# Denominators of two 512-token chunks in one TensorE burst, with reordered multiplications and five early final tiles

## The chip, the cores and the metric

The kernel runs on one core of a Trainium2 chip. The metric is device time in microseconds (us); the runs of one kernel agree within 0.4%.

Comparisons use a *stage length* read from the trace: from the start of the last burst of state products (its first matmul, at 313.99 us of the kernel before) to the start of the last matmul of the kernel.

## The reference

`x` is 2048 tokens of 1024 features. Branch A is linear attention with 32 heads of 32; branch B a dilated sliding-window softmax attention. The result is `g * A + (1 - g) * B`, with one gate `g` per token. What matters here is the end of branch A:

```python
pq, pk = phi(q), phi(k)                       # phi(t) = t+1 if t>0 else exp(t), + 1e-6
kv = einsum("bhsd,bhse->bhde", pk, v)
z = einsum("bhsd->bhd", pk)
num = einsum("bhqd,bhde->bhqe", pq, kv)
den = einsum("bhqd,bhd->bhq", pq, z)[..., None] + 1e-6
a = (num / den) @ wo
```

## The kernel before

A scheduler written in Python builds the kernel. Every operation is emitted with an estimated cost and a priority (by default its place in the order of emission); a list scheduler then fixes the order of the instructions of each engine, and semaphores are put where engines depend on each other. A wrong estimate therefore does not only delay one operation: whatever stands behind it on that engine waits too. The eight PSUM banks that the kernel uses are also handed out while operations are emitted.

In the last stage, `kv` and `wo` have been folded into one matrix, so a chunk of 512 tokens needs: eight groups of *numerators* (projection `q`, then `phi`, stored as `pq`), one burst of *denominators*, the reciprocal, eight multiplications of `pq` by it, and eight *output groups* (4 token tiles, two halves each). Then *final tiles* add branch B.

Some words that recur: a *plain group* is eight 128x512 matmuls of 128 rows and 128 columns (`128*128` in the traces) that add up in one PSUM bank. A *burst* is a run of *column-tiled* matmuls: `tile_position` gives each of four matmuls its own strip of 32 columns, and the four run side by side as one *wave* (in the traces they start 3 to 4 ns apart, and the next wave 0.216 to 0.227 us after them). A *PSUM move* reads a finished bank out on VectorE or ScalarE, so that the bank is free again; for a numerator it is the last step of `phi`.

```python
def over(u):                                  # denominators of chunk u
    tgt, c0 = pqn(u)
    db = main.next()                          # a PSUM bank
    def fn(e):
        for q in range(2):                    # two waves of four column-tiled matmuls
            for c in range(4):
                last = e.matmul(db.ap()[32*c:32*c+32, :], zsel[:, 2*c+q, :], tgt[:, 2*c+q, c0:c0+512],
                                start=(q == 0), stop=(q == 1), tile_position=(0, 32*c), ...)
        return last
    P.op("pe", fn, 0.55, mode="c", ...)
    # ACT: R = exp(-ln(den));  SP: 4 stores of R to HBM
    for j in range(8):
        B, bs = RBr.next()                    # ring of 12 buffers
        # SP: load the reciprocals back, spread over partitions
        P.op("sp", ..., chan="rci%d" % bs, lat=1.0)
        P.op("dve", ... tensor_tensor(dst, dst, B, mult), 0.65, ...)
# ... cut ...
for n, (u, j) in enumerate(nums):             # 4 chunks x 8 numerators
    numer(u, j)
    if j == 7:
        after(3, lambda u=u: over(u))
    slot(0)
    if n in (2, 4, 6, 8):
        fold((n - 2) // 4, (n - 2) // 2 % 2)
    if n >= 20:
        a_out(*outs.pop(0))                   # output groups between numerators
        slot(0)
# ... cut ...
EARLY = 3
for t in range(EARLY):
    while len(outs) > 8:
        a_out(*outs.pop(0))
    final(t)
while outs:
    a_out(*outs.pop(0))
```

## Time and profile before

| | before |
|---|---|
| time, median of 6 runs | 488.48 us (488.10 to 489.16) |
| span of the profiled execution, granted clock | 486.2 us, 0.999 |
| TensorE (PE) busy | 98% |
| stage length | 168.895 us |
| denominator bursts | 4 of 8 matmuls |

The page of the kernel before: span, busy times of the engines, two rows of the 40 slices (busy tenths), and the chain that ended last, by engine.

```profile
span 486.2 us, 10107 instructions
PE 474.9 (98%) x4336; PEld 222.2 (46%) x4403; DVE 288.4 (59%) x557; ACT 139.0 (29%) x225; POOL 5.5 (1%) x34
...
PE   8999999999999999999999999999999999999997
...
DVE  2112336899788888575666656596865735434444
...
PE 95%; DVE 2%; issue 1%; DMA 1%; SPq 0%; ACT 0%; DVEq 0%
```

PE is full from the first slice to the last, and the chain is PE. (The records of matmuls overlap: one of a plain group is shown as 0.379 us long, and the next starts 0.216 us after its start. Therefore I do not rest on the 98% but on the starts, every 0.216 us.)

The timeline of PE around the first two denominator bursts; columns are start, duration, engine, line, operation, out<-in, shapes, count. L1626 is the denominator, L1599 a fold, L1333 any plain group.

```profile
329.76 0.43 PE L1599 MATMUL ps_all<-w,kvT 32*32 32x512 bf16 x16
330.36 1.67 PE L1333 MATMUL ps_all<-xT,w 128*128 128x512 bf16 x7 [0.16 <-issue]
331.96 0.61 PE L1626 MATMUL ps_all<-pq,zsel 128*32 128x512 bf16 x8
...
348.15 0.62 PE L1626 MATMUL ps_all<-xT,zsel 128*32 128x512 bf16 x8
348.70 3.63 PE L1333 MATMUL ps_all<-xT,w 128*128 128x512 bf16 x15
```

The burst at 331.96 has two waves, and the next group starts at 332.51. From the single records: 0.309 us from the last plain matmul to the first wave, 0.548 us from there to the next plain group, whose second matmul follows after 0.227 us. If a wave took no more than the step of a plain group, eight matmuls in two waves would take 2 x 0.216 us (an estimate).

What PE waited for in the last stage (columns: waiter, cause, total us, times, longest us):

```profile
PE ps_all L1333 <- issue: 0.3, 2, 0.2
```

So nothing but "issue", and 0.3 us of it.

### The profile page before, as it was taken

The numbers are of one execution on the slowest core, as the hardware profiler recorded it, in microseconds if no ns is written. First come the engines' busy times: TensorE is split into PE (matmuls) and PEld (weight loads), VectorE is DVE, ScalarE is ACT, GpSimd is POOL, SyncE is SP. The second block draws the span as 40 slices with busy tenths as digits, with TensorE's granted clock in tenths as the row PEclk, the third lists the DMA queues.
The fourth block names the chain that finished last, engine by engine and source line by source line (L and its number), as shares of the span: only waits on it lengthen the run. The fifth ranks groups of instructions, "written<-read, shape, count | busy, mean of one in ns | idle before, by whom it ended". The sixth has DMA issues, their size and how long they took to land.

```text
span 486.2 us, 10107 instructions
## 1 busy us (share of the span) xinstructions
PE 474.9 (98%) x4336; PEld 222.2 (46%) x4403; DVE 288.4 (59%) x557; ACT 139.0 (29%) x225; POOL 5.5 (1%) x34
## 2 busy tenths in 40 slices
PE   8999999999999999999999999999999999999997
PEld 3444444444444444444444544444444444444443
DVE  2112336899788888575666656596865735434444
ACT  2111111214322233324534333455423322010000
POOL 4000000000000000000000000000000000000000
PEclk9999999999999999999999999999999999999999
DMA  8999992222014459423312322822674316101212
GB/s 221 225 208 309 357 361 63 85 89 87 2 43 142 106 153 233 99 77 84 77 44 65 98 55 48 200 51 41 160 190 98 99 17 179 43 24 44 88 67 89
DMA packets 72951, 57.39 MB, mean 118 GB/s; under 512 B 37953, under 2 KB 60865, under 8 KB 72898
## 3 DMA queue, kind: packets, MB, share of 16 engines
q1 hardware_dynamic: 72210, 56.07, 43.1%
q8 instruction: 36, 0.59, 0.5%
q10 hardware_dynamic: 688, 0.59, 0.4%
q14 instruction: 17, 0.14, 0.1%
HBM read 34.49 MB, written 13.76 MB: 99 GB/s over the span
## 4 chain that ended last, share of the span: by engine, by line
PE 95%; DVE 2%; issue 1%; DMA 1%; SPq 0%; ACT 0%; DVEq 0%
PE ps_all L1333 78%; PE ps_all L1675 11%; PE ps_all L1462 2%; PE ps_all L1439 2%; DMA xT<-in_A_x_dram 1%; PE ps_all L1547 1%; DVE zsel L1589 1%; PE ps_all L1626 0%; DVE pq L1346 0%; SPq L1307 0%; PE ps_all L1599 0%; SPq L1312 0%; DVE rs L1471 0%; DVE e L1344 0%; ACT e L1340 0%
## 5 line engine op out<-in xcount | busy, mean ns | idle before, releaser
L1333 PE MATMUL ps_all<-w,xT 128*128 128x512 bf16 x921 | 209.1, 379 | 4.6 <-issue 1.9
L1333 PE MATMUL ps_all<-xT,w 128*128 128x512 bf16 x747 | 168.3, 379 | 2.0 <-issue 1.3
L1333 PEld LDWEIGHTS ps_all<-w,xT 128*128 128x128 bf16 x960 | 91.1, 98 | 109.6 <-DMA xT<-in_A_x_dram 1.8
L1333 PEld LDWEIGHTS ps_all<-xT,w 128*128 128x128 bf16 x768 | 73.7, 98 | 89.0 <-issue 1.8
L1675 PE MATMUL ps_all<-w,qT 128*128 128x512 bf16 (+1 forms) x259 | 55.3, 372 | 0.3
L1675 PEld LDWEIGHTS ps_all<-w,qT 128*128 128x128 bf16 x264 | 25.8, 98 | 29.7
L1364 DVE CAST vst<-ps_all 128x512 bf16<-128x512 f32 x15 | 10.4, 694 | 43.1 <-PE ps_all L1333 43.1
L1447 ACT ACTIVATE E<-ps_all 128x1824 bf16<-128x1824 f32 (+1 forms) x18 | 30.4, 1687 | 13.4 <-PE ps_all L1439 13.4
L1344 DVE TENSOR_SCALAR e<-e 128x512 bf16<-128x512 bf16 x64 | 17.9, 283 | 26.6 <-ACT e L1342 15.6
L1679 DVE SCALAR_TENSOR_TENSOR o<-ps_all,gm,xT 128x512 bf16<-128x512 f32 (+1 forms) x25 | 18.1, 729 | 23.1 <-PE ps_all L1675 22.9
L1342 ACT ACTIVATE e<-ps_all 128x512 bf16<-128x512 f32 x32 | 19.1, 597 | 42.8 <-PE ps_all L1333 42.8
L1340 ACT ACTIVATE e<-ps_all 128x512 bf16<-128x512 f32 x32 | 19.1, 597 | 36.1 <-PE ps_all L1333 35.3
L1294 DVE TENSOR_TENSOR mx<-mx,kT 128x1024 bf16<-128x1024 bf16 x32 | 20.7, 686 | 9.3 <-ACT kT L1365 9.2
L1294 DVE TENSOR_TENSOR mx<-mx,qT 128x1024 bf16<-128x1024 bf16 x32 | 20.8, 686 | 6.6 <-ACT qT L1368 6.6
L1365 ACT ACTIVATE az<-ps_all 128x512 bf16<-128x512 f32 x22 | 13.2, 599 | 38.3 <-PE ps_all L1333 38.3
L1365 ACT ACTIVATE vst<-ps_all 128x512 bf16<-128x512 f32 x17 | 10.2, 599 | 47.5 <-PE ps_all L1333 47.5
L1473 DVE TENSOR_TENSOR ot<-ps_all,rs 128x512 bf16<-128x512 f32 x36 | 23.6, 683 | 0.2 <-DVE rs L1471 0.2
L1450 DVE TENSOR_TENSOR E<-E,msk 128x1824 bf16<-128x1824 bf16 (+1 forms) x18 | 19.9, 1103 | 5.8 <-ACT E L1447 5.2
L1346 DVE SCALAR_TENSOR_TENSOR pk<-ps_all,e 128x512 bf16<-128x512 f32 x32 | 21.9, 687 | 0.6
L1365 ACT ACTIVATE kT<-ps_all 128x512 bf16<-128x512 f32 x17 | 10.1, 597 | 39.8 <-PE ps_all L1333 39.8
L1368 ACT ACTIVATE qT<-ps_all 128x512 bf16<-128x512 f32 x17 | 10.1, 597 | 39.0 <-PE ps_all L1333 38.9
L1642 DVE TENSOR_TENSOR xT<-xT,rb 128x512 bf16<-128x512 bf16 x24 | 16.3, 688 | 8.5 <-DMA rb<-rc_hbm 8.4
(72 smaller groups left out, 259.1 us busy)
## 6 DMA issues: line engine op xcount, KB each, us to landing
rb<-rc_hbm SPq DMA_DIRECT2D x32, 256.0 KB, 5.0
w<-in_A_wqkv_dram SPq DMA_DIRECT2D x6, 1024.0 KB, 8.6
v<-vB_hbm SPq DMA_DIRECT2D x36, 132.0 KB, 3.0
vB_hbm<-vst SPq DMA_DIRECT2D x32, 132.0 KB, 6.2
w<-in_B_wqkv_dram SPq DMA_DIRECT2D x4, 1024.0 KB, 8.6
xn<-in_A_x_dram SPq DMA_DIRECT2D x16, 256.0 KB, 2.8
out_dram<-o SPq DMA_DIRECT2D x15, 256.0 KB, 2.1
oB_hbm<-ot SPq DMA_DIRECT2D x36, 96.0 KB, 2.1
```

The source lines that it names most:

```text
L1294: P.op("dve", lambda e, m=m, op=op: e.tensor_tensor(m[:, 0:n], m[:, 0:n], src, op), 0.08 + n / 1920.0, reads=[m.all(), reg], writes=[m.all()],
L1333: last = e.matmul(bank.ap(), lhs(dc), rhs(dc), start=(dc == 0), stop=(dc == 7))
L1340: P.op("act", lambda e: e.activation(e_[:, :], bank.ap(), ACT.Exp), act(512), reads=[bank.iv], writes=[e_.all()])
L1342: P.op("act", lambda e: e.activation(e_[:, :], bank.ap(), ACT.Exp, accum_out=qe[:, col:col + 1]), act(512) + 0.1, reads=[bank.iv], writes= ...
L1344: P.op("dve", lambda e: e.tensor_scalar(e_[:, :], e_[:, :], 1.0, 1e-6, op0=ALU.min, op1=ALU.add), 0.25, reads=[e_.all()], writes=[e_.all()])
L1346: P.op("dve", lambda e: e.scalar_tensor_tensor(out=dst, in0=bank.ap(), scalar=0.0, in1=e_[:, :], op0=ALU.max, op1=ALU.add), dps(512), read ...
L1365: fa = lambda e: e.activation(dst, src(), ACT.Copy)
L1447: P.op("act", lambda e: e.activation(E[:, 0:32 * nq].rearrange("p (j q) -> p j q", j=4), ps[:, 4:8, 0:8 * nq], ACT.Exp), act(32 * nq), rea ...
L1450: P.op("dve", lambda e: e.tensor_tensor(ev(), ev(), m[:, :, :].rearrange("p r q -> p (r q)")[:, None, :].to_broadcast([128, 16, 2 * nq]), ...
L1473: P.op("dve", lambda e, r=r, bv=bv, h=h: e.tensor_tensor(o[:, 512 * h:512 * h + 512].rearrange("p (k i c) -> p k i c", k=2, c=32), bv()[:, ...
L1675: last = e.matmul(bank.ap(0, f1 - f0), qT[:, dc, t * 128:(t + 1) * 128], ws[3][:, dc, f0:f1], start=(dc == 0), stop=(dc == 7))
L1679: P.op("dve", lambda e, bank=bank, o_=o_, t=t, n=n, i0=i0, i1=i1, tgt=tgt, c0=c0: e.scalar_tensor_tensor(out=o_[:, i0 * 128:i1 * 128].rear ...
```

## The change

Its intent: two chunks' denominators in one burst, which halves the number of switches between plain and column-tiled matmuls; because the second chunk's reciprocals then come later, multiplications get a lower priority than PSUM moves, the cost model of the reciprocal loads is changed, and five final tiles (three before) are emitted ahead of the output groups of chunks 2 and 3, as work for PE meanwhile.

```diff
-        def over(u):
+        def over(*us):
+            dbs = [main.next() for _ in us]
+            def fn(e):
+                for u, db in zip(us, dbs):
+                    tgt, c0 = pqn(u)
+                    ... the same 2 x 4 matmuls for each chunk ...
+            P.op("pe", fn, 0.1 + 0.45 * len(us), mode="c", ...)
+            for u, db in zip(us, dbs):
+                spread(u, db)          # Ln, Exp, stores, loads, multiplications
...
-                                  chan="rci%d" % bs, lat=1.0)
+                                  chan="rci%d" % bs, lat=0.6, pad=4.0)      # pad was 2.0 for every DMA
-                P.op("dve", ... ALU.mult), 0.65, reads=[reg, B.all()], writes=[reg])
+                P.op("dve", ... ALU.mult), 0.65, reads=[reg, B.all()], writes=[reg],
+                     prio=1000 + len(P.ops) + (120 if u % 2 else 80))
...
-            if j == 7:
-                after(3, lambda u=u: over(u))
+            if j == 7 and u % 2:
+                after(3, lambda u=u: over(u - 1, u))
...
-        EARLY = 3
+        EARLY = 5
         for t in range(EARLY):
-            while len(outs) > 8:
+            while len(outs) > 16:
```

I call the four parts *pair*, *load model*, *priority* and *early tiles*.

More of the change, by code (lines that the diff above doesn't have):

```diff
@@ L59 @@
 class Op:
-    __slots__ = ("eng", "fn", "cost", "deps", "prio", "seq", "chan", "lat", "pos", "val", "users", "raw", "name", "mode", "start", "end")
+    __slots__ = ("eng", "fn", "cost", "deps", "prio", "seq", "chan", "lat", "pos", "val", "users", "raw", "name", "mode", "pad", "start", "end")
 class Prog:
@@ L78, in __init__, with op @@
         self.read = set()
-    def op(self, eng, fn, cost, reads=(), writes=(), prio=None, chan=None, lat=0.0, after=(), name="", mode="m"):
+    def op(self, eng, fn, cost, reads=(), writes=(), prio=None, chan=None, lat=0.0, after=(), name="", mode="m", pad=2.0):
         o = Op()
+        o.pad = pad
         o.eng, o.fn, o.cost, o.prio, o.chan, o.lat, o.name, o.mode = eng, fn, cost, prio, chan, lat, name, mode
@@ L188, in schedule @@
                 dma_free = max(dma_free, o.end) + o.lat
-                fin = dma_free + 2.0
+                fin = dma_free + o.pad
             o.pos = len(self.order[e])
@@ L1617, in plan, with spread @@
         last_in = [None]
-        def over(u):
-            tgt, c0 = pqn(u)
-            db = main.next()
-            def fn(e):
-                for q in range(2):
-                    for c in range(4):
-                        last = e.matmul(db.ap()[32 * c:32 * c + 32, :], zsel[:, 2 * c + q, :], tgt[:, 2 * c + q, c0:c0 + 512], start=(q == 0), stop=(q == 1),
-                                        tile_position=(0, 32 * c), skip_group_check=True)
-                return last
-            P.op("pe", fn, 0.55, mode="c", reads=[zsel.all(), tgt.part((0, 8), (c0, c0 + 512))], writes=[db.iv], name="den")
+        def over(*us):
[3 more added lines that the diff above has]
+                    tgt, c0 = pqn(u)
+                    for q in range(2):
+                        for c in range(4):
+                            last = e.matmul(db.ap()[32 * c:32 * c + 32, :], zsel[:, 2 * c + q, :], tgt[:, 2 * c + q, c0:c0 + 512], start=(q == 0), stop=(q == 1),
+                                            tile_position=(0, 32 * c), skip_group_check=True)
+                return last
+            P.op("pe", fn, 0.1 + 0.45 * len(us), mode="c", reads=[zsel.all()] + [t.part((0, 8), (c, c + 512)) for t, c in map(pqn, us)], writes=[db.iv for db in dbs], name="den")
+            for u, db in zip(us, dbs):
+                spread(u, db)
+        def spread(u, db):
+            tgt, c0 = pqn(u)
             R, rs = RAr.next()
@@ L1639, in over @@
                 last_in[0] = P.op("sp", lambda e, B=B, src=src: e.dma_start(B[:, :], src), 0.5, reads=[[("R", 4 * u + j // 2, 4 * u + j // 2 + 1, None)]], writes=[B.all()],
-                                  chan="rci%d" % bs, lat=1.0)
+                                  chan="rci%d" % bs, lat=0.6, pad=4.0)
                 dst, reg = tgt[:, j, c0:c0 + 512], tgt.part((j, j + 1), (c0, c0 + 512))
-                P.op("dve", lambda e, B=B, dst=dst: e.tensor_tensor(dst, dst, B[:, :], ALU.mult), 0.65, reads=[reg, B.all()], writes=[reg])
+                P.op("dve", lambda e, B=B, dst=dst: e.tensor_tensor(dst, dst, B[:, :], ALU.mult), 0.65, reads=[reg, B.all()], writes=[reg],
+                     prio=1000 + len(P.ops) + (120 if u % 2 else 80))
         def a_loc(t):
```

## The prediction

> **What bounds the kernel.** TensorE. The page has PE busy 98% of the 486.2 us span; the chain of waits is 95% PE; the granted clock is 0.999. In the stage that the change touches (314 to 483 us: numerators, denominators, output of A, final output) the waits of PE list only 0.3 us. A 128x512 matmul starts every 0.216 us; 31 numerators, 32 output groups of A and 248 full plus 16 half final matmuls make about 164 us, four denominator bursts and four folds about 4 us, of 168.9 us. So about 1 us is not streaming, nearly all at changes between full-array and tiled matmuls.
>
> **What the change removes.** Two of four denominator bursts merge into the other two. In the order of time each burst starts 0.309 us after the matmul before it, its two waves stand 0.216 us apart, and the next group starts 0.312 us later, then 0.226 instead of 0.216 us. Against 0.216 us steps, entering and leaving costs 0.20 us per burst. [...] Two bursts fewer save about 0.4 us on the critical chain.
>
> **What it moves.** No matmul, multiplication or byte is removed: 32 multiplications at 0.69 us [...], 4 Ln, 4 Exp, 16 stores and 32 loads of reciprocals remain. VectorE is 63% busy from 322 to 414 us; letting PSUM moves go first frees banks earlier, but PE is not waiting for banks now: worth nothing.
>
> **What could be lost.** Today a chunk is multiplied 17.3 us after its burst (332.0 to 349.3; 394.4 to 411.8). The burst of chunks 0 and 1 will come near 348 us. SyncE needs 0.8 us per store and 0.73 to 0.87 us per load; I estimate chunk 0 ready 19 to 21 us after the burst, chunk 1 about 27 us. The numerators still to do then are about 13 x 1.73 = 23 us, so it fits with 3 us to spare, if the static order does not put an output group of chunk 0 earlier. The new load model (0.6 us steps, landing 5.1 us after issue) is right about the landing (5.0 us median) but optimistic about the steps, so PE may stall 0 to 3 us before the first output groups. The second burst comes about 376 us instead of 394; chunk 1's output groups and five final tiles (17 us) cover it. The tail (0.48 us VectorE, 2 us store) stays.
>
> **Predicted.** 0.4 us saved, a small stall expected at 0.2 us: 488.3 us, 8 in 10 between 487.4 and 490.0. Faster by over 2%: 0.01; within 2%: 0.97; slower: 0.02.
>
> **What the profile would show.** Right: 16 denominator matmuls in each of two bursts about 0.97 us long, no waits of PE in the last stage, first burst near 348 us, last multiplication before today's 411.8 us, PE's end 0.4 us earlier. Wrong: PE waits for a multiplication before an output group of chunk 0 or 2, or for a bank held by a late PSUM move because VectorE in its fixed order sits on a late load; or output stores sit behind reciprocal loads in SyncE's order (12 buffers for 16 loads), so that the two output buffers run out.
>
> **What would make it wrong.** Multiplications 10 us later than the numerators' end; or a different static order in the earlier stages (the scheduler keeps the best of six passes), which I expect to change only tenths.

The 0.69 us of a multiplication is read from the trace of the kernel before.

## The result

| | before | changed |
|---|---|---|
| time, median of 6 runs | 488.48 us (488.10 to 489.16) | 487.75 us (487.28 to 488.02) |
| ratio, 95% interval | | 0.9983 (0.9970 to 0.9996) |
| span of the profiled execution | 486.2 us | 486.1 us |
| stage length | 168.895 us | 168.444 us |
| denominator bursts | 4 of 8 | 2 of 16 |

Ratios here are the mean time of one kernel's runs over that of the kernel before in the same rounds, so not quite the ratio of the medians.

The page after has the same shape:

```profile
span 486.1 us, 10113 instructions
PE 474.5 (98%) x4336; PEld 222.3 (46%) x4403; DVE 290.0 (60%) x560; ACT 137.1 (28%) x222; POOL 5.5 (1%) x34
...
PE 93%; SPq 2%; DVE 2%; issue 1%; DMA 1%; ACT 0%; DVEq 0%
```

The timeline of PE around the first burst, and around the second. L1628 is now the denominator, L1600 the fold, L1334 a plain group, L1683 a final tile; `xT,w` are numerators, `w,pq` and `w,xT` output groups.

```profile
330.20 0.43 PE L1600 MATMUL ps_all<-w,kvT 32*32 32x512 bf16 x16
330.80 15.49 PE L1334 MATMUL ps_all<-xT,w 128*128 128x512 bf16 x70 [0.16 <-issue]
346.21 0.62 PE L1628 MATMUL ps_all<-pq,zsel 128*32 128x512 bf16 x8
346.66 0.60 PE L1628 MATMUL ps_all<-xT,zsel 128*32 128x512 bf16 x8
347.19 22.62 PE L1334 MATMUL ps_all<-xT,w 128*128 128x512 bf16 x102
369.65 2.54 PE L1334 MATMUL ps_all<-w,pq 128*128 128x512 bf16 x10
```

```profile
388.64 1.89 PE L1334 MATMUL ps_all<-xT,w 128*128 128x512 bf16 x8
390.37 3.62 PE L1334 MATMUL ps_all<-w,xT 128*128 128x512 bf16 x15
393.92 1.05 PE L1628 MATMUL ps_all<-xT,zsel 128*32 128x512 bf16 x16
394.90 5.35 PE L1334 MATMUL ps_all<-w,xT 128*128 128x512 bf16 x24
400.09 17.43 PE L1683 MATMUL ps_all<-w,qT 128*128 128x512 bf16 x78
417.35 22.83 PE L1334 MATMUL ps_all<-w,xT 128*128 128x512 bf16 x103
```

The first burst lasts from 346.21 to 347.19, 0.98 us for four waves. Nine numerators stand between the last fold and it, and thirteen (102 recorded matmuls) after it; then come output groups of chunk 0. Eleven of these precede the last numerator, so the second burst starts only at 393.92. PE has no wait besides the same "issue" (and not even that in a second trace of the same kernel, whose matmul records are complete):

```profile
PE ps_all L1334 <- issue: 0.3, 2, 0.2
```

The instruction order of all five engines is the same in both kernels until the first burst of the kernel before (332 us). From 129 us to the last state burst both take 184.8 us. What differs in the traces is therefore the last stage, by 0.451 us. In these two profiled executions a slower start (124.01 against 123.25 us to the first score) hid it from the spans.

Two groups of lines of VectorE (DVE) show how close the rest runs; L1649 is the multiplication, L1347 and L1345 are `phi`, L1687 the final addition. (The view names the type of the first operand only; the reciprocals `rb` are fp32 in `kernel.py`.)

```profile
366.36 0.69 DVE L1347 SCALAR_TENSOR_TENSOR xT<-ps_all,e 128x512 bf16<-128x512 f32 x1
366.96 0.69 DVE L1649 TENSOR_TENSOR pq<-pq,rb 128x512 bf16<-128x512 bf16 x1
...
412.98 0.69 DVE L1649 TENSOR_TENSOR xT<-xT,rb 128x512 bf16<-128x512 bf16 x1 [0.26 <-DMA rb<-rc_hbm]
414.39 0.69 DVE L1649 TENSOR_TENSOR xT<-xT,rb 128x512 bf16<-128x512 bf16 x1 [0.71 <-DMA rb<-rc_hbm]
417.63 1.41 DVE L1687 SCALAR_TENSOR_TENSOR o<-ps_all,gm,pq 128x512 bf16<-128x512 f32 x2 [2.55 <-DMA out_dram<-o]
```

The last multiplication of chunk 0 ends at 367.65, 21.4 us after its burst, and PE wants chunk 0 at 369.65: 2.0 us to spare. At 417.63 DVE had sat 2.55 us on an output store (there are only two output buffers), but PE did not feel it.

### The profile page after: what moved, and what is told of

It reads as the page before. It is cut to its first block, busy times and chain, and to the rows that moved or that the text cites. A ratio compares the mean times of both kernels' runs of the same rounds, so it can differ in the third digit from the quotient of the medians.

```text
span 486.1 us, 10113 instructions
## 1 busy us (share of the span) xinstructions
PE 474.5 (98%) x4336; PEld 222.3 (46%) x4403; DVE 290.0 (60%) x560; ACT 137.1 (28%) x222; POOL 5.5 (1%) x34
## 4 chain that ended last, share of the span: by engine, by line
PE 93%; SPq 2%; DVE 2%; issue 1%; DMA 1%; ACT 0%; DVEq 0%
PE ps_all L1334 76%; PE ps_all L1683 11%; PE ps_all L1463 2%; PE ps_all L1440 2%; SPq L1308 1%; DMA w<-in_B_wqkv_dram 1%; PE ps_all L1548 1%; DVE zsel L1590 1%; SPq L1313 1%; PE ps_all L1628 0%; DVE pq L1347 0%; PE ps_all L1600 0%; DVE rs L1472 0%; DVE e L1345 0%; ACT e L1341 0%
## 5 line engine op out<-in xcount | busy, mean ns | idle before, releaser
L1334 PE MATMUL ps_all<-w,xT 128*128 128x512 bf16 x922 | 208.9, 379 | 5.0 <-issue 1.9
L1334 PE MATMUL ps_all<-xT,w 128*128 128x512 bf16 x746 | 166.5, 379 | 2.0 <-issue 1.3
L1334 PEld LDWEIGHTS ps_all<-w,xT 128*128 128x128 bf16 x960 | 91.0, 98 | 110.4 <-DMA w<-in_B_wqkv_dram 1.7
L1334 PEld LDWEIGHTS ps_all<-xT,w 128*128 128x128 bf16 x768 | 73.8, 98 | 88.8 <-issue 1.3
L1683 PE MATMUL ps_all<-w,qT 128*128 128x512 bf16 (+1 forms) x259 | 55.3, 372 | 0.3
L1683 PEld LDWEIGHTS ps_all<-w,qT 128*128 128x128 bf16 x264 | 25.8, 98 | 29.7
L1345 DVE TENSOR_SCALAR e<-e 128x512 bf16<-128x512 bf16 x64 | 18.1, 285 | 25.6 <-ACT e L1343 14.5
L1687 DVE SCALAR_TENSOR_TENSOR o<-ps_all,gm,xT 128x512 bf16<-128x512 f32 (+1 forms) x25 | 18.1, 729 | 21.1 <-PE ps_all L1683 20.9
L1366 ACT ACTIVATE vst<-ps_all 128x512 bf16<-128x512 f32 x17 | 10.2, 600 | 48.0 <-PE ps_all L1334 48.0
L1347 DVE SCALAR_TENSOR_TENSOR pk<-ps_all,e 128x512 bf16<-128x512 f32 x32 | 21.9, 688 | 0.6
L1366 ACT ACTIVATE kT<-ps_all 128x512 bf16<-128x512 f32 x17 | 10.2, 598 | 39.8 <-PE ps_all L1334 39.8
L1369 ACT ACTIVATE qT<-ps_all 128x512 bf16<-128x512 f32 x17 | 10.2, 598 | 39.0 <-PE ps_all L1334 38.9
L1430 DVE TENSOR_SCALAR qd<-qT,par 128x912 bf16<-128x912 bf16 (+1 forms) x33 | 14.3, 453 | 11.1 <-PE ps_all L1440 11.1
```

What stands on the lines that cost most here:

```text
L1334: last = e.matmul(bank.ap(), lhs(dc), rhs(dc), start=(dc == 0), stop=(dc == 7))
L1345: P.op("dve", lambda e: e.tensor_scalar(e_[:, :], e_[:, :], 1.0, 1e-6, op0=ALU.min, op1=ALU.add), 0.25, reads=[e_.all()], writes=[e_.all()])
L1347: P.op("dve", lambda e: e.scalar_tensor_tensor(out=dst, in0=bank.ap(), scalar=0.0, in1=e_[:, :], op0=ALU.max, op1=ALU.add), dps(512), read ...
L1366: fa = lambda e: e.activation(dst, src(), ACT.Copy)
L1683: last = e.matmul(bank.ap(0, f1 - f0), qT[:, dc, t * 128:(t + 1) * 128], ws[3][:, dc, f0:f1], start=(dc == 0), stop=(dc == 7))
L1687: P.op("dve", lambda e, bank=bank, o_=o_, t=t, n=n, i0=i0, i1=i1, tgt=tgt, c0=c0: e.scalar_tensor_tensor(out=o_[:, i0 * 128:i1 * 128].rear ...
```

## The experiments

The first question was where the 0.45 us come from: from the two bursts that are gone, or from the new order of the other work. The theory: each burst has a fixed cost of entering and leaving, and nothing else matters. The rival: the order of multiplications, PSUM moves and final tiles.

### Four bursts again, everything else kept

```diff
-                after(3, lambda u=u: over(u - 1, u))
+                after(3, lambda u=u: over(u - 1))
+                after(4, lambda u=u: over(u))      # each burst also depends on the last plain group emitted
...
         while later:
             slot(0)
+            if later:
+                a_out(*outs.pop(0))                # the group between the bursts of the second pair
```

> The changed kernel, but the two chunks of a pair are parted by one ordinary matmul group: four bursts of 8 again, everything else of the change kept. Measure: time from the start of the last state burst to the start of the last matmul (before 168.90 us, changed kernel 168.44 us). Theory (each burst costs a fixed entry and exit of 0.20 us, the gain is two of them): 168.88 us, that is, the whole gain is gone. Rival (the gain comes from the new order of multiplications, moves and final tiles): stays at 168.44 us.

Stage 168.882 us; time 488.37 us, ratio to the kernel before 0.9999 (0.9985 to 1.0013). The gain is gone. PE around the first pair:

```profile
346.34 0.62 PE L1631 MATMUL ps_all<-pq,zsel 128*32 128x512 bf16 x8
346.89 1.90 PE L1336 MATMUL ps_all<-xT,w 128*128 128x512 bf16 x8
348.72 0.62 PE L1631 MATMUL ps_all<-xT,zsel 128*32 128x512 bf16 x8
349.27 4.92 PE L1336 MATMUL ps_all<-xT,w 128*128 128x512 bf16 x21
```

Two bursts of 0.55 us with one group between, in place of one of 0.98 us. The rival falls for the size of the gain.

### Eight bursts

```diff
-                after(3, lambda u=u: over(u - 1, u))
+                for i in range(4):
+                    after(3 + i, lambda u=u, i=i: half(u - 1 + i // 2, i % 2))   # one wave of 4 matmuls each
... half() itself and the output groups between the bursts are cut here ...
```

> The changed kernel with each burst cut into single waves of 4 matmuls, an ordinary group between them: eight bursts. Theory: a lone wave costs 0.309 + 0.312 + 0.010 - 0.216 = 0.415 us, 8 x 0.415 = 3.32 us against 2.17 us for two bursts of 16: stage 169.59 us, time about 1.15 us above the changed kernel. Rival (order of the other work): 168.44 us.

Stage 169.764 us; time 489.12 us, ratio 1.0023 (1.0009 to 1.0037). The effect has the direction and form of the theory; it is 0.17 us over the expected number, because I had taken 0.312 us as the way out of a lone wave. The records show 0.332 us from a wave's first matmul to the next group. The fixed cost of a burst is then 0.309 + 0.332 + 0.011 - 2 x 0.216 = 0.220 us (in, last wave and out, the slow second matmul, less two ordinary steps). Two, four and eight bursts should stand 2 x 0.220 = 0.44 and 6 x 0.220 = 1.32 us apart from the changed kernel; measured 0.438 and 1.320 us.

### The other three parts without the pair

```diff
-            if j == 7 and u % 2:
-                after(3, lambda u=u: over(u - 1, u))
+            if j == 7:
+                after(3, lambda u=u: over(u))
```

> Only the other parts of the change (load model, later multiplications, five final tiles up), one chunk per burst as before. Theory: stage 168.88 to 168.90 us, no gain over the kernel before. Rival: 168.44 us or less.

Stage 168.881 us; time 488.64 us, ratio 1.0000 (0.9986 to 1.0014). As expected: alone they are worth nothing.

### The pair without the other three parts

```diff
 load model, priority and EARLY as in the kernel before; only over(u - 1, u)
```

> Only the merged bursts; load model, order of multiplications and three final tiles as before. Theory: stage 168.44 us if PE meets no wait; the blind prediction feared 0 to 3 us of wait before the first output groups, which would show as PE waiting for a multiplication. Rival: 168.9 us.

This missed widely: 504.69 us, ratio 1.0333 (1.0319 to 1.0347), stage 186.206 us. What PE waited for in the last stage, and the timeline around the second burst:

```profile
PE ps_all L1334 <- DVE xT L1649: 14.0, 1, 14.0
PE ps_all L1334 <- DVE xT L1347: 0.5, 2, 0.3
PE ps_all L1334 <- DVE pq L1649: 0.3, 1, 0.3
```

```profile
395.00 1.05 PE L1628 MATMUL ps_all<-xT,zsel 128*32 128x512 bf16 x16
395.99 5.35 PE L1334 MATMUL ps_all<-w,xT 128*128 128x512 bf16 x24
415.31 2.74 PE L1334 MATMUL ps_all<-w,xT 128*128 128x512 bf16 x6 [13.97 <-DVE xT L1649]
431.41 8.80 PE L1682 MATMUL ps_all<-w,qT 128*128 128x512 bf16 x40
```

Three output groups after the burst, PE reaches chunk 2 and stands still for 14 us until its multiplications are done; the final tiles that could have filled the time (L1682) come 16 us later. The stretches from 401.0 and 415.3 us, with the columns start:end, length, then busy time of PE, PEld, DVE, ACT, POOL, granted clock, DMA share, GB/s:

```profile
401.00:415.30 14.30, 0.34 (x2) 0.00 (x0) 6.29 (x9) 0.69 (x1) 0.00 (x0) 0.69 0.86 221
415.30:420.00 4.70, 4.47 (x11) 1.67 (x13) 2.85 (x5) 0.00 (x0) 0.00 (x0) 0.51 1.07 272
```

The granted clock falls from 1.00 (380 to 401 us) to 0.69 in the first stretch and 0.51 in the second, and the next eleven steps from matmul to matmul are mostly 0.427 us instead of 0.216. (The slow steps last 4.7 us here, and 4.1, 3.3 and 2.9 us after the three other long waits below; for the last two the granted clock was 0.54 from 365.6 to 369.2 us and 0.57 from 438 to 441 us.) The excess over ordinary steps is 14.1 us in the wait, 2.3 us in slow matmuls after it, and 1.3 us in three small gaps at 361 to 366 us, together 17.7 us of the 17.76 us above the changed kernel.

So the other parts are not idle decoration. Which of them keeps the pair from stalling?

### The changed kernel without the early tiles

```diff
-        EARLY = 5
+        EARLY = 3
-            while len(outs) > 16:
+            while len(outs) > 8:
```

> The changed kernel without the five final tiles moved up (three again, after all but 8 output groups, as before). In the run of merged bursts alone PE waited 14.0 us for a multiplication of chunk 2 at the second burst, with 11 output groups put before the first final tile. Theory (that part alone makes the wait, because the output groups and final tiles take their PSUM banks in the order of emission): wait of 14 us again, stage 168.44 + about 17 = 185 to 186 us. Rival (the load model or the later multiplications cured it): no wait, 168.44 us.

503.29 us (one look), stage 184.082 us, 1 to 2 us less than expected, as the three small gaps (1.3 us) are absent here. The wait is back, and it is the only one:

```profile
PE ps_all L1334 <- DVE xT L1649: 13.5, 1, 13.5
```

The gap is 13.68 us over an ordinary step and the slow matmuls after it cost 1.95 us: 15.63 us of the 15.64 us above the changed kernel. PE's order is again eleven output groups after the second burst and then final tiles. That this is so because late-emitted final tiles must take banks from these output groups is read from the code; shown is that this part alone, present or absent, decides about the wait. Whether the number of early tiles or their place does it was not run apart.

### Pair and early tiles, without load model and priority

```diff
 load model and priority as in the kernel before; EARLY = 5 and over(u - 1, u) kept
```

> Merged bursts and the five final tiles moved up, but the old load model and the multiplications in their old priority. Theory: no 14 us wait; only the small waits around the first burst that the run of merged bursts alone showed between 361 and 366 us (0.20 + 0.34 us for numerators' PSUM moves behind multiplications, 0.29 us for a multiplication) remain: stage 168.44 + 0.8 = 169.3 us. Rival (load model and priority do nothing): 168.44 us.

489.18 us, ratio 1.0017 (1.0001 to 1.0032), stage 169.684 us, 1.24 us above the changed kernel and 0.4 us more than expected. Three gaps at 361 to 366 us account for 1.20 us of it: 0.882, 0.483 and 0.486 us where 0.216 is usual. The one that is long enough to be listed:

```profile
PE ps_all L1334 <- DVE xT L1347: 0.5, 1, 0.5
```

PE waits for the numerators' PSUM moves (L1347), which stand behind multiplications on DVE. The 0.45 us gain would have turned into a loss.

### The changed kernel without the priority, and without the load model

```diff
-                     prio=1000 + len(P.ops) + (120 if u % 2 else 80))      # first run: no priority
```
```diff
-                                  chan="rci%d" % bs, lat=0.6, pad=4.0)
+                                  chan="rci%d" % bs, lat=1.0)              # second run: old load model
```

> The changed kernel with the multiplications in their old priority (new load model and five final tiles kept). With both old, PE lost 1.24 us at 361 to 366 us (gaps of 0.88, 0.48 and 0.49 us where 0.22 is usual). Theory A (the priority of PSUM moves over multiplications removes these waits): stage 169.4 to 169.7 us. Theory B (the load model does it, since the old one places a multiplication on VectorE 2 us before its data land): stage 168.44 us.

> The changed kernel with the old load model (new priority and five final tiles kept). Theory A (priority): stage 168.44 us. Theory B (load model): 169.4 to 169.7 us, with VectorE waiting 2 us for the first reciprocal load.

Without the load model: stage 168.448 us (487.57 us, one look). Nothing is lost. Without the priority: 498.00 us (one look), stage 178.633 us, far more than either theory said. Theory A has the right part and too small a size. PE's waits in the last stage, and DVE from 357 us on (L1649 multiplications, the bracket gives the idle time before and its cause):

```profile
PE ps_all L1334 <- DVE o L1686: 3.8, 1, 3.8
PE ps_all L1334 <- DVE pq L1649: 3.2, 1, 3.2
```

```profile
357.68 0.69 DVE L1649 TENSOR_TENSOR pq<-pq,rb 128x512 bf16<-128x512 bf16 x1 [0.31 <-DMA rb<-rc_hbm]
358.61 0.69 DVE L1649 TENSOR_TENSOR pq<-pq,rb 128x512 bf16<-128x512 bf16 x1 [0.24 <-DMA rb<-rc_hbm]
...
364.13 1.49 DVE L1649 TENSOR_TENSOR pq<-pq,rb 128x512 bf16<-128x512 bf16 x2 [0.23 <-DMA rb<-rc_hbm]
365.54 0.28 DVE L1345 TENSOR_SCALAR e<-e 128x512 bf16<-128x512 bf16 x1
```

DVE now goes from one reciprocal load to the next and does nothing else until 365.54, although the Exp of the next numerator was done at 358.0 us and its `phi` steps could have followed. And because the scheduler believed in earlier multiplications, it let only nine numerators follow the burst (thirteen in the changed kernel); PE came to chunk 0 at 362 us and waited to 365.68. The second wait is on a final addition that sat on an output store, which landed 10.9 us after it was issued (the median of its kind is 2.3 us). Why so late was not tested, but the traces point to one cause. Just before this store, at 424.79 us, SyncE issues the write of 512 single maxima (`mx_hbm<-mx`), and the read that waits for this write starts only at 435.94 us; the store lands at 437.06 us. Elsewhere too a store that is issued during this write lands right after it (at 431.28 us after 431.10 us with pair and early tiles only, at 430.42 us after 430.21 us with the old load model). The changed kernel has such a store of 10.0 us as well, and PE did not feel it. Waits of 3.34 and 3.92 us, and slow-clock matmuls after them of 1.60 and 1.34 us, make 10.20 us of the 10.19 us.

### The changed kernel once more

> The changed kernel once more, to settle its size against the kernel before. The stage says -0.45 us (ratio 0.9991); the first measurement said 0.9983 (0.997 to 0.9996). Theory: 0.9991 within its interval, stage 168.44 us.

487.55 us, ratio 0.9984 (0.9971 to 0.9998), stage 168.447 us. Both times the ratio says about 0.8 us, the stage 0.45 us (ratio 0.9991); each interval includes that. Taken together, the single times (11 runs against 15) give 0.85 us with an interval of 0.6 to 1.1 us, so a gain beyond the stage is likely. The record shows where 0.18 us of it lies: outside the profiled span. Time less span averages 1.94 us for the kernel before and 1.76 us for the changed one (standard deviations 0.08 and 0.03 us). The bursts are not its cause: it is 2.10 us with four bursts again and 1.74 us for the other three parts alone. Some 0.2 us remain that I cannot tell from the scatter of the start.

### The same idea for the state products, and the folds

The state products (`kv`) of 16 token tiles are column-tiled bursts too, 16 of 32 matmuls. I joined two tiles to a burst, adding up in PSUM, with three instead of two buffers for both operands:

```diff
-                if r == 3:
-                    states.append((slot_n[0] + 4, lambda ...: state(t, pkt, azt)))
+                if r == 3 and t % 2:
+                    states.append((slot_n[0] + 4, lambda ...: state(t, two)))    # start=(k == 0), stop=(k == 1)
```

> The changed kernel, with the same idea where it was not tried: the state products of two token tiles in one column-tiled burst that adds up in PSUM (three buffers instead of two for each operand), 8 bursts instead of 16. Theory: a burst on its own costs 0.415 us now, one next to the attention values 0.309 us, of which I estimate 0.11 us is streaming; 5 + 11 bursts become 2 + 6. From the first score matmul to the last matmul 353.27 us becomes 351.4 us (-1.3 to -1.9), time about 1.5 us under the changed kernel. Rival (PE waits for the third buffer or for one of its four banks and gives it back): 353.3 us or more.

487.41 us, ratio 0.9982 (0.9968 to 0.9996); first score to last matmul 353.327 us against 353.285 us of the changed kernel: no gain. There are two reasons. A burst of 64 lasts 0.597 us to the next group and one of 32 lasts 0.311 us, so 32 more matmuls cost 0.286 us, not my estimate of 0.11 (eight sets of 33 columns at the rate of a plain matmul would be 264/512 x 0.216 us = 0.11 us): joining saves less, as more of a burst is its matmuls than I had thought. And the rest of the saving was given back by a wait in the folds (L1606):

```profile
317.70 3.63 PE L1335 MATMUL ps_all<-xT,w 128*128 128x512 bf16 x16
321.84 0.44 PE L1606 MATMUL ps_all<-w,kvT 32*32 32x512 bf16 x16 [0.52 <-DVE pq L1348]
322.21 3.63 PE L1335 MATMUL ps_all<-xT,w 128*128 128x512 bf16 x16
```

The second fold takes four PSUM banks that DVE frees late. It has a smaller wait of the same place in the changed kernel (0.438 us from the matmul before instead of 0.309 us). Spreading the folds removes it:

```diff
-            if n in (2, 4, 6, 8):
-                fold((n - 2) // 4, (n - 2) // 2 % 2)
+            if n in (3, 6, 9, 12):
+                fold((n - 3) // 6, (n - 3) // 3 % 2)
```

> The changed kernel with the four folds after numerators 3, 6, 9 and 12 instead of 2, 4, 6 and 8. The second fold started 0.438 us after the matmul before it, the others 0.309 us: it waits for PSUM banks that VectorE frees late. Theory: the 0.13 us go, stage 168.31 us. Rival (the gap is something of the fold itself): 168.44 us.

> State bursts in pairs together with the spaced folds. In the run of paired state bursts these bursts took 0.48 us less, but the second fold waited 0.46 us more than usual 0.438 us for VectorE, and one burst 0.09 us. Theory: without that wait the saving stays: first score matmul to last matmul 353.33 - 0.59 = 352.7 us against 353.27 us of the changed kernel, about 0.5 us less time. Rival (another wait takes it back): 353.2 us or more.

Spaced folds alone: stage 168.314 us (487.46 us, one look), 0.13 us less as expected, and all four folds start after 0.309 us. Both together: first score to last matmul 352.715 us, 0.57 us less than the changed kernel, as expected; 487.24 us, ratio to the kernel before 0.9966 (0.9952 to 0.9980). By the trace this version beats both kernels; its time was not measured in one call with the changed kernel, whose ratio was 0.9983 and 0.9984.

## Why the prediction was right, point by point

- *About the total*: right. Predicted 488.3 us (487.4 to 490.0), measured 487.75 us, within 2% as given 0.97. This says little by itself: a gain of 0.45 us in 488 could hardly leave that range, so the mechanism has to be judged by the points below.
- *"Two bursts fewer save about 0.4 us on the critical chain"*: right in mechanism, and shown by two, four and eight bursts. The size is 0.44 us, since a burst's fixed cost is 0.220 us; I had read 0.20 us and left out two times 0.01 us inside the waves. What TensorE does at a change between plain and tiled matmuls is not shown: the trace has only the gaps, 0.309 us into a burst and 0.322 us from its last wave to the next group.
- *"a small stall expected at 0.2 us"*: did not come. PE has no new wait in the last stage. With 0.44 us and no stall the sum would have been 488.1 us against the 488.56 us that I started from (the median of the three runs that I had then). The times say about 0.8 us and the stage 0.45 us; of the rest 0.18 us lies outside the profiled span, by a cause that is open, and about 0.2 us may be chance.
- *"letting PSUM moves go first ... worth nothing"*: this step was wrong for the changed kernel. It is true of the kernel before (the other parts alone gave 168.881 us), but with pairs the priority is worth 10.2 us, and still about 1.2 us when the old load model is used. I judged a part by the waits of the old order and not by what the new order would put on DVE.
- *"I estimate chunk 0 ready 19 to 21 us after the burst, chunk 1 about 27 us"*: chunk 0 took 21.4 us, and 2.0 us were to spare where I had said 3. The risk that I named, an output group of chunk 0 placed earlier, is what happened without the priority.
- *"The new load model is ... optimistic about the steps, so PE may stall"*: the load model made no difference once the priority was there (168.448 us).
- *"The second burst comes about 376 us"* and *"last multiplication before today's 411.8 us"*: wrong. The second burst came at 393.9 us, as eleven output groups went ahead of the last numerator, and multiplications ran until 426.9 us. It cost nothing, as output groups and five final tiles did cover it; that this cover is needed is shown by the 13.5 us wait without it. That it also covered a burst 18 us later than I had assumed was luck. Of the signs that I had named for "wrong", one did appear without cost: DVE sat 2.55 us on an output store because the two output buffers had run out.

## What to carry to other kernels

On a saturated TensorE, count the changes between plain and tiled matmuls and multiply by the measured cost of one; merging the denominators paid exactly that here (0.438 us for two bursts of 0.220 us), while merging the state bursts, which are longer in matmuls, paid less. When merging makes data arrive later, look in the new fixed order for what every engine will do in the meantime: here two parts that gain nothing by themselves, the priority and the early tiles, decide between 0.45 us won and 0.8 to 17.3 us lost against the kernel before. And a long wait on TensorE can cost more than itself: the four waits of 3.3 us and more in these runs were each followed by 1.3 to 2.3 us lost in slow matmuls, while after gaps of up to 0.9 us none followed (with the pair alone the granted clock was 1.00 from 361 to 369.2 us, around three small gaps).

## What else the traces showed

- In these runs a column-tiled burst of 128x512 matmuls between plain groups cost 0.220 us beyond its waves (two, four and eight bursts: 168.444, 168.882, 169.764 us).
- In the state bursts, 33 columns wide and four tiles side by side, 32 more matmuls took 0.286 us, 36 ns for a set of four; the records put the first eight sets of a joined burst about 25 ns apart and the next eight about 34 ns.
- Matmul records can be missing from a trace. In the kernel before, 43 of 49 plain runs after a tiled burst are one matmul short of a multiple of 8 (the lines with x15 and x7 after a fold or a burst), mostly by one of the first three records, and the 0.16 us "issue" waits (20, together 3.2 us) stand at such places: the record at 330.36 starts 0.543 us after the fold's last record where complete runs show 0.317 us, just one step more. The trace of the changed kernel once more settles it. It has 4403 matmul records, where the first trace of the same kernel has 4336; all its 47 plain runs after a tiled burst are complete, and from 129 us to the end it lists no wait of PE at all. These "issue" waits are thus no idle time.
